# Attention units fed into an expert layer: x read back into the masks' ring, keys a step later, side work by an average

## The chip, the cores and the metric

One core of a Trainium2 chip runs the kernel. The metric is the device time of one execution, in microseconds; the time before is the median of three runs. Every duration below that isn't a run's time comes from one profiled execution.

## The reference

A gated linear attention over 4 batches, 8 heads, 768 positions and head size 48 is followed by two expert layers, all in f32:

```
f = sigmoid(f_logit)
state[t] = f[t] * state[t-1] + outer(k[t], v[t])       # per batch and head, 48 x 48
y[t] = q[t] @ state[t]
x = y as (3072, 384)
xn = x / sqrt(mean(x*x) + 1e-6) * rms_g
x3 = (silu(xn @ w_gate) * (xn @ w_val)) @ w_out         # 384 -> 1536 -> 384
out = relu(x3 @ w_in)**2 @ w2_out                       # 384 -> 2048 -> 384
```

## The kernel before

The attention is cut into 24 **units**: unit u is 128 positions of one batch, all 8 heads; `units` counts the batches first, so the state of a batch is needed again four units later. Four units make a group of 512 tokens, for which the first expert layer (`phase1`) runs once. Products in f32 are made of three matmuls each (`mm3`): an operand is split into a high and a low part ("h" and "l" in the names).

`first` computes units 0 to 7 and the expert layer of group 0 in an order written out by hand. Then `phase1` runs groups gi = 1 to 5. A group has 12 hidden blocks f, and each has three **steps**: a G step (9 matmuls for the gate, tile `g`), a V step (9 for the value, tile `v`) and an O step (9 of the output product of the block before, tiles `acc`). Step s of the whole stage is 36 gi + 3 f + 0, 1 or 2. With the G step ACT computes the silu (`si`, tile `sg`), with the V step DVE multiplies v into `sg` (`vs`) and ACT makes the high part `hh`, with the O step DVE makes the low part `hl`. `g` and `v` have one bank of PSUM each.

During the steps of group gi the units of group gi + 1 are prepared. `segment(s)` issues, after the matmuls of step s, first the functions of the dictionary `side` at s, then the step's own work (`si`; `vs` and `hh`; or `hl`), then the PE functions of `tail` at s. Each engine runs its instructions in the order in which they were issued. `plan_unit(u, s)` puts the parts of unit u at offsets from its start s:

- `load_gates`, `load_v`, `load_qk` ask for the unit's inputs on SP. `gate` (ACT, L296 and L297) makes sigmoids of the gates; `scan_b` (DVE, L308 and L309) and `scan_a` (DVE, L316) their running products; `mul_k` (L319) and `mul_q` (L322) multiply them into keys and queries.
- `scores` (PE, L341, tile `sc`) needs both products. `masked` (DVE, L360) writes the two masked tiles `sm`, from a ring of four buffers with the tag "sm", and `attend` (PE, L449 and L461) makes y from them and the state.
- `k_turn` (DVE, L395) transposes keys in blocks and stores them to memory (`kd`); `k_back` reads them back with their blocks swapped, `kcopy` (ACT, L436) copies them to `ktok`, `kv` (PE, L476) multiplies them with v, and `state_add` (DVE, L492) adds that to the state, which `decay` (ACT, L330) has scaled. Units 20 to 23 are the last of their batches and have none of these but `decay`.
- `norm` (ACT) and `power` (POOL) give the scale of the RMS norm, `x_scale` (DVE, L404) applies it, `x_turn` (DVE, L409) transposes in blocks and stores (`xd`, L383), `x_back` reads it back with four reads (L388), and `x_high` (ACT, L423) and `x_low` (DVE, L427) split it into `xh` and `xl`, the input of the group's G and V steps.

Beside that, the weights of the second expert layer are converted, summed and split (`w2_load`, `w2_scale`, `w2_bits`, `w2_sum`, `w2_part`, `w2_plain`) and stored to memory. `plan_work` puts these pieces into `side`, in their order, each into the first step in which DVE and ACT have room by the table `COST`: planned microseconds of a step may reach `CAP`, plus what `room` grants for the PE work of the attention in that step. In group 5, which has no units to prepare, the last weights are split, then `open_late` and `x3_load` (L1045) fetch weights and the first layer's results for the second layer (`phase2`), and `x_split` (ACT, L1086; DVE, L1087) and `x_sum` prepare them. The three copies of `acc` of a finished group (`evac_x3`, ACT, L903) take buffers of the tag "sm" too.

The ring of `qk` tiles has two buffers; a unit's x is read back into the place of its keys, so the buffer is held until `x_low`:

```
def x_back(u):
    block_read(u, "xd", block_view(U[u]["k"], KT))
```

Of the kernel before, what the change touches and what calls it, by code (L numbers as in the profile page):

```python
# [8 lines left out]
F32 = mybir.dt.float32  # L9
# [7 lines left out]
P = 128  # L17
# [5 lines left out]
KT = DM // P  # L23
# [4 lines left out]
UG = 4  # L28
# [161 lines left out]
def tile_linear_attention_moe(  # L190
# [16 lines left out]
    def pool(name, stack=main, **kw):  # L207
        return stack.enter_context(tc.tile_pool(name=name, **kw))
# [7 lines left out]
    ap_ = pool("attn", upper, bufs=2, reuse_waits="tile")  # L216
# [36 lines left out]
    def flat(x):  # L253
        return x.rearrange("p a t -> p (a t)")


    U = {}
# [117 lines left out]
    BL = 4  # L375

    def block_view(x, n):
        return flat(x)[:, 0:BL * n * 32].rearrange("p (b n j) -> p b n j", b=BL, n=n)
# [6 lines left out]
    def block_read(u, nm, to):  # L385
        src = U[u][nm].rearrange("(a i) c n j -> c i a (n j)", a=BL)
        for c in range(BL):
            nc.sync.dma_start(to[32 * c:32 * c + 32].rearrange("i a n j -> i a (n j)"), src[c])  # L388
        U[u][nm + "o"] = to
# [22 lines left out]
        block_write(u, "xd", t)  # L412

    def x_back(u):
        block_read(u, "xd", block_view(U[u]["k"], KT))

    def x_part(t, u):
        return t[:, :, u % UG * C:(u % UG + 1) * C].rearrange("p k (c i) -> p k c i", c=BL)
# [252 lines left out]
    def w2_plain(key, nm, a, b):  # L671
        if nm not in w2t:
            w2t[nm] = w2_tile(nm)
        w2_split(key, w2f[key], w2t[nm][:, a], w2t[nm][:, b])
# [37 lines left out]
    def w2_part(i, c):  # L712
        t, b = w2c[i, c]
        w2_split(("c", i, c), t[:, b], t[:, 2 + b], t[:, b])

    def w2_spare(i, key):
        t, _ = w2c[i, 2]
        w2_split(key, w2f[key], t[:, 1], t[:, 3])
# [31 lines left out]
    side, tail, planned, room = {}, {}, {}, {}  # L750
    TAIL = dict(scores=0.9, attend=1.3, kv=0.3)

    def at(where, s, fn):
        where.setdefault(max(s, NG), []).append(fn)

    starts = {}

    def plan_unit(u, s):
        starts[u] = s
        for k, fns in (  # L760
            (-9, (load_gates, load_v)), (max(-9, starts.get(u - 2, 0) + 10 - s), (load_qk,)), (-3, (gate,)), (-2, (scan_b, keep_end)), (-1, (scan_a, mul_k)),
            (0, (mul_q, k_turn, decay)), (1, (masked,)), (2, (k_back,)), (3, (norm, power)), (4, (kcopy, x_scale)),
            (5, (x_turn,)), (6, (state_add,)), (7, (x_back,)), (9, (x_high, x_low)),
        ):
            for fn in fns:
                if fn not in (load_gates, load_qk, load_v) or u > 2 * UG:
                    at(side, s + k, lambda fn=fn: fn(u))
                    planned.setdefault(s + k, []).append(fn.__name__)
        for k, fn in ((0, scores), (2, attend), (5, kv)):
            at(tail, s + k, lambda fn=fn: fn(u))  # L770
            room[s + k] = room.get(s + k, 0) + TAIL[fn.__name__]

    NG = 3 * F1
    for gi in range(1, NU - 1):
        for j in range(UG):
            plan_unit((gi + 1) * UG + j, gi * NG + ((4, 11, 19, 26) if gi == 1 else (-1, 8, 17, 26))[j])
    COST = dict(
        scan_b=(1.4, 0), keep_end=(0, 0.2), scan_a=(1.2, 0), mul_k=(0.7, 0), mul_q=(0.7, 0), masked=(1.4, 0),
        k_turn=(0.6, 0), kcopy=(0, 0.6), gate=(0, 2.2), decay=(0, 1.5), norm=(0, 1.0), x_scale=(0.5, 0), x_turn=(0.5, 0),
        state_add=(0.7, 0), x_high=(0, 0.5), x_low=(0.5, 0),  # L780
    )
    load = {}
    CAP = 2.1

    def busy(s):
        if s not in load:
            b = [(0.0, 0.6), (0.7, 0.6), (0.7, 0.0)][s % 3]
            load[s] = list(b)
        return load[s]

    for s, names in planned.items():
        for nm in names:
# [5 lines left out]
    def job(name, fn, dve=0.0, act=0.0, after=()):  # L798
        work.append((name, fn, (dve, act), after))

    def conversion(pair, after=()):
        job(("load", pair), lambda: w2_load(pair), after=after)

    def bits(pair, after=()):
        job(("scale", pair), lambda: w2_scale(pair), act=0.9, after=((("load", pair), 3),) + after)
        for n, c in enumerate((0.55, 0.96, 0.96)):
            job(("bits", pair, n), lambda n=n: w2_bits(pair, n), dve=c, after=((("scale", pair), 1),))

    def sums(i, cs, after=()):
        for n, x in enumerate(W_SUMS[cs]):  # L810
            act = x[1] == "="
            job(("sum", i, cs, n), lambda n=n: w2_sum(i, cs, n), dve=0 if act else 0.3, act=0.3 if act else 0, after=after)

    def split(name, fn, after=()):
        job(name, fn, dve=0.56, act=0.51, after=after)

    def plan_work():
        gone = ()
        for i in range(F2 // 3):
            a = tuple(("a", 3 * i + f) for f in range(3))  # L820
            b = tuple(("b", 3 * i + f) for f in range(3))
            pa, pb, pc = (a[0], a[1]), (a[2], b[0]), (b[1], b[2])
            if i == 0:
                conversion(pa)
                conversion(pb)
            bits(pa)
            bits(pb)
            sums(i, (0, 1))
            for c in (0, 1):
                split(("part", i, c), lambda i=i, c=c: w2_part(i, c), ((("sum", i, (0, 1), 5), 1),))  # L830
            sums(i, (2,))
            split(("part", i, 2), lambda i=i: w2_part(i, 2), ((("sum", i, (2,), 3), 1),))
            split(("plain", b[0]), lambda i=i, k=b[0]: w2_spare(i, k))
            sums(i, (3, 4), after=((("part", i, 1), 2),))
            conversion(pc, after=((("plain", b[0]), 2),))
            for c in (3, 4):
                split(("part", i, c), lambda i=i, c=c: w2_part(i, c), ((("sum", i, (3, 4), 5), 1),))
            bits(pc)
            if i + 1 < F2 // 3:
                na, nb = (("a", 3 * i + 3), ("a", 3 * i + 4)), (("a", 3 * i + 5), ("b", 3 * i + 3))  # L840
            else:
                na, nb = (("a", F2 - 1), ("b", F2 - 1)), None
            for n, k in enumerate(pc):
                split(("plain", k), lambda k=k, n=n, nm=f"b{3 * i + 1}": w2_plain(k, nm, 2 * n, 2 * n + 1))
                if n == 0:
                    conversion(na, after=((("bits", pc, 2), 1),))
            if nb:
                conversion(nb, after=((("plain", pc[1]), 2),))
        bits(na)
        for n, k in enumerate(na):  # L850
            split(("plain", k), lambda k=k, n=n: w2_plain(k, "last", 2 * n, 2 * n + 1))
        job(("open",), open_late, after=((("plain", na[1]), 1), (None, last0 + 2)))
        job(("x3",), lambda: (x3_tiles(), x3_load(0)), after=((None, last0 + 9),))
        freed = [2, 6, 8, 12, 14, 18, 20, 24, 26, 30, 32, 36]
        for n, p in enumerate(X_KEYS):
            f = next(f for f, c in enumerate(freed) if c >= n + 4)
            at_least = ((None, last0 + 3 * (f + 1) + 3), (("x3",), 3))
            for q in X_NEEDS.get(p, ()):
                job(("xsum", q), lambda q=q: x_sum(q, r_tile(f"xs_{q}")), dve=0.56, after=at_least)
            split(("x", p), lambda p=p: (x_tile(p), x_split(p)))  # L860
            work[-1] = work[-1][:3] + (at_least,)

        for b in range(10):
            f = next(f for f, c in enumerate(freed) if c >= b + 21)
            job(("b", b), lambda b=b: fetch_b(b), after=((None, last0 + 3 * (f + 1) + 3),))

        for name, fn, cost, after in work:
            s = max([NG, when.get("last", 0)] + [when[a] + g if a else g for a, g in after])
            while any(busy(s)[e] + c > CAP + room.get(s, 0) and c for e, c in enumerate(cost)):
                s += 1  # L870
            for e, c in enumerate(cost):
                busy(s)[e] += c
            when[name] = when["last"] = s
            at(side, s, fn)
# [161 lines left out]
    def x3_tiles():  # L1036
        L["x3"] = [wp.tile([P, 2, NT], F32, tag="w", name=f"x3_{k}") for k in range(KT)]

    def x3_load(s):
        o, g = 2 * NT * s, 0  # L1040
        while g < 2 * NT:
            gi, c = divmod(o + g, N)
            n = min(N - c, 2 * NT - g)
            for k in range(KT):
                nc.sync.dma_start(  # L1045
                    L["x3"][k].rearrange("p a t -> p (a t)")[:, g:g + n], x3d[gi][:, k, c:c + n]
                )
            g += n
# [374 lines left out]
```

## Time and profile before

| what | value |
|---|---|
| median of three runs | 980.8 us (979.37 to 981.16) |
| the profiled execution's own time | 979.5 us |
| its span, first to last instruction | 977.7 us |
| PE busy | 927.1 us, 95% |
| DVE busy | 646.3 us, 66% |
| ACT busy | 489.4 us, 50% |
| POOL busy | 31.6 us, 3% |
| mean granted clock of TensorE | 0.989 |

The span has four stretches: units 0 to 7 and group 0 of the first layer (to about 134 us), groups 1 to 4 with the units of groups 2 to 5 (to about 520 us), group 5 (to about 600 us), and the second layer. In the second layer PE is busy throughout. The start of a row is counted from the span's start.

### The profile page before, as it was taken

What the parts mean: (1) busy time and instruction counts of PE and PEld (TensorE: products, weight loads), DVE (VectorE), ACT (ScalarE), POOL (GpSimd) and SP (SyncE); (2) the same over time, 40 slices, a digit from 0 to 9 for tenths busy, and PEclk for the clock granted to TensorE, in tenths of its full rate; (3) what the DMA queues carried; (4) which work ended last, traced back from release to release, by engine and by line L of the source; (5) the groups of instructions that cost most, each with busy time, mean ns of one, the idle gap of its engine ahead of it and who ended that gap; (6) DMA issues with size and microseconds to landing.
All of it is one profiled execution on the core that took longest, in us unless ns stands there. A gap on an engine that the chain in (4) does not pass through costs nothing.

```text
span 977.7 us, 15776 instructions
## 1 busy us (share of the span) xinstructions
PE 927.1 (95%) x5945; PEld 813.0 (83%) x5945; DVE 646.3 (66%) x1147; ACT 489.4 (50%) x1020; POOL 31.6 (3%) x54
## 2 busy tenths in 40 slices
PE   6799999999899999998999799999999999999997
PEld 4578877877777777776777688999999999999997
DVE  6899967676666676765665354767675767667552
ACT  5877653444443544443434233556554655555451
POOL 3210000000000000000000000000000000000000
PEclk8999999999999999999999999999999999999999
DMA  9556443466456457446234425842464165406400
GB/s 322 181 184 209 150 165 103 122 195 187 130 170 220 133 175 230 123 150 208 75 114 162 178 97 184 287 141 75 137 194 148 39 206 159 146 12 182 129 25 28
DMA packets 78387, 148.48 MB, mean 152 GB/s; under 512 B 17248, under 2 KB 44000, under 8 KB 78304
## 3 DMA queue, kind: packets, MB, share of 16 engines
q1 hardware_dynamic: 78304, 147.39, 46.6%
q8 instruction: 49, 0.80, 0.3%
q14 instruction: 34, 0.28, 0.1%
HBM read 115.12 MB, written 32.24 MB: 151 GB/s over the span
## 4 chain that ended last, share of the span: by engine, by line
PE 87%; issue 3%; DMA 2%; DVE 2%; ACT 2%; SPq 0%; ACTq 0%; DVEq 0%
PE o L730 7%; PE o L729 7%; PE o L728 7%; PE X L1099 7%; PE Y L1099 5%; PE acc L728 5%; PE g L728 5%; PE g L729 5%; PE g L730 5%; PE acc L729 5%; PE acc L730 5%; PE v L728 5%; PE v L730 4%; PE v L729 4%; PE sc L341 2%
## 5 line engine op out<-in xcount | busy, mean ns | idle before, releaser
L730 PE MATMUL o<-wb,h 128*128 128x384 f32 x384 | 128.6, 335 | 0.0
L728 PE MATMUL o<-wb,h 128*128 128x384 f32 x384 | 128.3, 334 | 0.0
L729 PE MATMUL o<-wb,h 128*128 128x384 f32 x384 | 128.3, 334 | 0.0
L968 ACT CAST hh<-sg 128x512 fp32r<-128x512 f32 x72 | 44.6, 619 | 108.5 <-DVE sg L965 108.4
L960 ACT ACTIVATE sg<-g 128x512 f32<-128x512 f32 x72 | 42.7, 594 | 97.9 <-PE g L730 97.8
L965 DVE TENSOR_TENSOR sg<-v,sg 128x512 f32<-128x512 f32 x72 | 49.5, 688 | 61.2 <-PE v L730 60.8
L1099 PE MATMUL X<-xc,wa 128*128 128x384 f32 x360 | 82.5, 336 | 0.0
L730 PEld LDWEIGHTS o<-wb,h 128*128 128x128 f32 x384 | 72.1, 188 | 0.5
L728 PEld LDWEIGHTS o<-wb,h 128*128 128x128 f32 x384 | 72.1, 188 | 0.0
L729 PEld LDWEIGHTS o<-wb,h 128*128 128x128 f32 x384 | 72.1, 188 | 0.0
L1099 PE MATMUL Y<-xc,wa 128*128 128x384 f32 x300 | 68.3, 335 | 0.0
L1099 PEld LDWEIGHTS X<-xc,wa 128*128 128x128 f32 x360 | 63.8, 188 | 1.8 <-ACT d L1174 1.2
L1178 DVE TENSOR_TENSOR c<-T,c 128x384 f32<-128x384 f32 x40 | 22.3, 558 | 52.8 <-PE T L1099 43.6
L970 DVE TENSOR_TENSOR hl<-sg,hh 128x512 fp32r<-128x512 f32 x72 | 49.2, 683 | 10.2 <-ACT hh L968 9.8
L1099 PEld LDWEIGHTS Y<-xc,wa 128*128 128x128 f32 x300 | 53.3, 188 | 0.7 <-DVE c L1178 0.6
L728 PE MATMUL g<-xh,wh_o 128*128 128x512 f32 x108 | 45.2, 419 | 6.0 <-ACT sg L960 6.0
L1129 DVE TENSOR_TENSOR h<-d,h 128x384 fp32r<-128x384 f32 x60 | 32.8, 554 | 26.2 <-ACT h L1128 25.9
L341 PE MATMUL sc<-qk 64*128 64x128 f32 x320 | 23.5, 285 | 26.2 <-issue 25.1
L341 PEld LDWEIGHTS sc<-qk 64*128 64x128 f32 x320 | 20.0, 188 | 33.5 <-issue 31.9
L1128 ACT CAST h<-d 128x384 fp32r<-128x384 f32 x60 | 30.2, 511 | 34.4 <-PE o L730 34.4
L1174 ACT COPY d<-X 128x384 f32<-128x384 f32 x40 | 19.1, 478 | 54.7 <-PE X L1099 54.7
L728 PE MATMUL acc<-hh,wh_o 128*128 128x512 f32 x108 | 44.0, 407 | 0.0
(192 smaller groups left out, 2286.9 us busy)
## 6 DMA issues: line engine op xcount, KB each, us to landing
wa<-w2d_c SPq DMA_DIRECT2D x100, 384.0 KB, 3.4
raw<-in_w_dram SPq DMA_DIRECT2D x18, 768.0 KB, 4.3
ff<-in_ff_dram SPq DMA_DIRECT2D x20, 516.0 KB, 4.6
qk<-in_qk_dram SPq DMA_DIRECT2D x20, 512.0 KB, 5.9
w2d_c<-ws_c SPq DMA_DIRECT2D x50, 192.0 KB, 4.5
raw_a<-in_w_dram SPq DMA_DIRECT2D x22, 384.0 KB, 4.2
wb<-w2d_b SPq DMA_DIRECT2D x16, 384.0 KB, 3.6
v<-in_vp_dram SPq DMA_DIRECT2D x24, 192.0 KB, 4.5
```

Of the source, the lines that this page charges most:

```text
L341: nc.tensor.matmul(U[u]["sc", hf][:, j], U[u]["k"][o:o + 64, j], U[u]["q"][o:o + 64, j], start=True, stop=True,)
L728: nc.tensor.matmul(o, lh, rh, start=first, stop=False)
L729: nc.tensor.matmul(o, lh, rl, start=False, stop=False)
L730: nc.tensor.matmul(o, ll, rh, start=False, stop=last)
L960: nc.scalar.activation(dd["s", f], dd["g", f], AF.Silu)
L965: nc.vector.tensor_mul(dd["s", f], dd["v", f], dd["s", f])
L968: nc.scalar.copy(dd["h", f][0], dd["s", f])
L970: nc.vector.tensor_sub(dd["h", f][1], dd["s", f], dd["h", f][0].bitcast(F32))
L1099: nc.tensor.matmul(o, w[a], x[:, b], start=first and n == 0, stop=last and n == 2, skip_group_check=True,)
L1128: nc.scalar.copy(t[:, 0], r)
L1129: later(lambda: nc.vector.tensor_sub(t[:, 1], r, t[:, 0].bitcast(F32)))
L1178: nc.vector.tensor_add(t, bk[b], t)
```

## The change

`x_back` reads into a tile of its own, the ring "sm" of the masks, one step earlier (start + 6 instead of + 7), and `x_high` and `x_low` use it one step later (+ 10 instead of + 9). `kcopy` moves from + 4 to + 5, `kv` from + 5 to + 6, `state_add` from + 6 to + 7. `load_v` and `load_qk` are bound to the start of the unit two before (+ 7 and + 9), whose buffers they take. The starts of the units move: in group 1 to 4, 11, 18, 24 (from 4, 11, 19, 26), in groups 2 to 4 to -3, 6, 15, 24 (from -1, 8, 17, 26). Some costs of the planner's table are changed by 0.05 to 0.1, `CAP` goes from 2.1 to 2.3, and `crowd` is new: a piece of side work is put into a step only if no six steps in a row that hold it pass 6 x 2.05 us plus their room.

```diff
     def x_back(u):
-        block_read(u, "xd", block_view(U[u]["k"], KT))
+        block_read(u, "xd", ap_.tile([P, BL, KT, 32], F32, tag="sm", name=f"xo{u}", bufs=4))
...
         for k, fns in (
-            (-9, (load_gates, load_v)), (max(-9, starts.get(u - 2, 0) + 10 - s), (load_qk,)), (-3, (gate,)), (-2, (scan_b, keep_end)), (-1, (scan_a, mul_k)),
-            (0, (mul_q, k_turn, decay)), (1, (masked,)), (2, (k_back,)), (3, (norm, power)), (4, (kcopy, x_scale)),
-            (5, (x_turn,)), (6, (state_add,)), (7, (x_back,)), (9, (x_high, x_low)),
+            (-9, (load_gates,)), (max(-9, starts.get(u - 2, 0) + 7 - s), (load_v,)),
+            (max(-9, starts.get(u - 2, 0) + 9 - s), (load_qk,)),
+            (-3, (gate,)), (-2, (scan_b, keep_end)), (-1, (scan_a, mul_k)),
+            (0, (mul_q, k_turn, decay)), (1, (masked,)), (2, (k_back,)), (3, (norm, power)), (4, (x_scale,)),
+            (5, (x_turn, kcopy)), (6, (x_back,)), (7, (state_add,)), (10, (x_high, x_low)),
         ):
...
-        for k, fn in ((0, scores), (2, attend), (5, kv)):
+        for k, fn in ((0, scores), (2, attend), (6, kv)):
...
-            plan_unit((gi + 1) * UG + j, gi * NG + ((4, 11, 19, 26) if gi == 1 else (-1, 8, 17, 26))[j])
+            plan_unit((gi + 1) * UG + j, gi * NG + ((4, 11, 18, 24) if gi == 1 else (-3, 6, 15, 24))[j])
...
-    CAP = 2.1
+    CAP, MEAN = 2.3, 2.05
...
+    def crowd(s, e):
+        near = [(sum(busy(t)[e] for t in range(b, b + 6)), sum(room.get(t, 0) for t in range(b, b + 6))) for b in range(s - 5, s + 1)]
+        return max(n - r - 6 * MEAN for n, r in near)
...
-            while any(busy(s)[e] + c > CAP + room.get(s, 0) and c for e, c in enumerate(cost)):
+            while any(c and (busy(s)[e] + c > CAP + room.get(s, 0) or crowd(s, e) + c > 0) for e, c in enumerate(cost)):
                 s += 1
```

What this does to the order shows around unit 19. First DVE, before: from `scan_b` of unit 19 to its `k_turn`. L965 is `vs`, L970 `hl`, L427 `x_low` of unit 18, L322 `mul_q` of unit 19.

```order
L308 SCALAR_TENSOR_TENSOR ff19_3817<-ff19_3817,floor_89 128x516
L309 RECIPROCAL seed_90<-ff19_3817 128x4
L316 SCALAR_TENSOR_TENSOR ff19_3817<-ff19_3817,seed_90 128x516
L319 TENSOR_TENSOR qk19_3846<-qk19_3846,ff19_3817 128x512
L965 TENSOR_TENSOR sg_3_8_4004<-v_3_8_4006,sg_3_8_4004 128x512
L427 TENSOR_TENSOR xl_1_4_3555<-qk18_3597,xh_1_4_3554 128x3x128
L322 TENSOR_TENSOR qk19_3846<-qk19_3846,ff19_3817 128x512
L395 STREAM_TRANSPOSE ff19_3817<-qk19_3846 128x4x4x32
```

And now, on the same engine, to the first mask of unit 19 (`vs` is L971 here, `hl` L976):

```order
L492 TENSOR_TENSOR state2_99<-kv18_3965,state2_99 48x4x48 x2
L308 SCALAR_TENSOR_TENSOR ff19_3788<-ff19_3788,floor_89 128x516
L309 RECIPROCAL seed_90<-ff19_3788 128x4
L971 TENSOR_TENSOR sg_3_7_3963<-v_3_7_3974,sg_3_7_3963 128x512
L316 SCALAR_TENSOR_TENSOR ff19_3788<-ff19_3788,seed_90 128x516
L319 TENSOR_TENSOR qk19_3792<-qk19_3792,ff19_3788 128x512
L976 TENSOR_TENSOR hl_3_7_3993<-sg_3_7_3963,hh_3_7_3992 128x512
L322 TENSOR_TENSOR qk19_3792<-qk19_3792,ff19_3788 128x512
L395 STREAM_TRANSPOSE ff19_3788<-qk19_3792 128x4x4x32
L561 TENSOR_SCALAR m_a9_3989<-m_a9_3989 128x768
L568 SCALAR_TENSOR_TENSOR m_a9_3989<-raw_a9_3902,m_a9_3989 128x768
L427 TENSOR_TENSOR xl_1_4_3587<-xo18_3953,xh_1_4_3586 128x3x128
```

`mul_q` stood behind the next `vs` and the `x_low` of unit 18; now `vs` comes two instructions sooner, `hl` stands between, and `x_low` has gone behind `mul_q`, reading the new tile xo18.

PE around the scores of unit 19 before: they follow the nine matmuls of an O step.

```order
L728 MATMUL acc_3_2_3490<-hh_3_7_3959,wh_v7_1055 128x512
L729 MATMUL acc_3_2_3490<-hl_3_7_3960,wh_v7_1055 128x512
L730 MATMUL acc_3_2_3490<-hh_3_7_3959,wl_v7_1056 128x512
L341 MATMUL sc19_0_4046<-qk19_3846 128x128
L341 MATMUL sc19_1_4047<-qk19_3846 128x128
```

And now, on PE: they follow the nine of the next G step.

```order
L728 MATMUL g_3_8_4007<-xh_1_3_2653,wh_g8_1062 128x512
L729 MATMUL g_3_8_4007<-xl_1_3_2654,wh_g8_1062 128x512
L730 MATMUL g_3_8_4007<-xh_1_3_2653,wl_g8_1063 128x512
L341 MATMUL sc19_0_4035<-qk19_3792 128x128
L341 MATMUL sc19_1_4036<-qk19_3792 128x128
```

Between the `vs` ahead of `mul_q` and the scores PE now has an O and a G step where it had an O step alone.

SP's queue round the returned x of unit 18, before: the store of x, a load of weights, the four reads.

```order
L383 DMA xd18_3953<-qk18_3597 128x384
L640 DMA raw_a11_3955<-in_w2_dram 128x768 x2
L388 DMA qk18_3597<-xd18_3953 32x4x96 x4
L383 DMA kd19_4035<-ff19_3817 128x512
L284 DMA ff20_4041<-in_ff_dram 128x1032
```

And now, on SP:

```order
L383 DMA xd18_3938<-qk18_3552 128x384
L388 DMA xo18_3953<-xd18_3938 32x4x96 x4
L640 DMA raw_a11_3960<-in_w2_dram 128x768 x2
L383 DMA kd19_4019<-ff19_3788 128x512
L284 DMA ff20_4025<-in_ff_dram 128x1032
```

The reads stand directly behind the store that they wait for, and the load of weights behind them.

## Rows read from the trace of the kernel before

**Rows 1.** The page: PE's busy time, share of the span and instructions.

```profile
PE 927.1 (95%) x5945; PEld 813.0 (83%) x5945; DVE 646.3 (66%) x1147; ACT 489.4 (50%) x1020; POOL 31.6 (3%) x54
```

**Rows 2.** Waits of PE, 130 to 600 us: total, times, longest.

```profile
PE sc L341 <- issue: 25.1, 14, 4.5
PE g L728 <- ACT sg L960: 5.2, 1, 5.2
PE sc L341 <- DVE qk L322: 1.2, 1, 1.2
```

**Rows 3.** The chain that ended last: start, length, what.

```profile
161.59 0.60 issue
...
200.85 0.60 issue
...
223.87 2.06 issue
...
442.32 4.45 issue
...
493.46 1.99 issue
```

**Rows 4.** Timeline of DVE, 389 to 399 us: start, length, instruction, idle before.

```profile
390.39 1.23 DVE L308 TENSOR_TENSOR_SCAN ff<-ff,floor 128x516 f32<-128x516 f32 x1 [1.46 <-ACT ff L297]
...
391.87 1.23 DVE L316 TENSOR_TENSOR_SCAN ff<-ff,seed 128x516 f32<-128x516 f32 x1
393.02 0.67 DVE L319 TENSOR_TENSOR qk<-qk,ff 128x512 f32<-128x512 f32 x1
393.72 0.69 DVE L965 TENSOR_TENSOR sg<-v,sg 128x512 f32<-128x512 f32 x1
395.51 0.56 DVE L427 TENSOR_TENSOR xl<-qk,xh 128x384 fp32r<-128x384 f32 x1 [1.10 <-ACT xh L423]
395.99 0.69 DVE L322 TENSOR_TENSOR qk<-qk,ff 128x512 f32<-128x512 f32 x1
...
397.34 0.65 DVE L970 TENSOR_TENSOR hl<-sg,hh 128x512 fp32r<-128x512 f32 x1
397.94 1.29 DVE L360 TENSOR_TENSOR sm<-sc,mask 128x512 f32<-128x512 f32 x2
```

**Rows 5.** Timeline of ACT, the same stretch.

```profile
394.44 0.62 ACT L968 CAST hh<-sg 128x512 fp32r<-128x512 f32 x1 [1.30 <-DVE sg L965]
394.97 0.51 ACT L423 CAST xh<-qk 128x384 fp32r<-128x384 f32 x1
```

**Rows 6.** Timeline of PE, the same stretch: V, O, scores of unit 19.

```profile
391.40 0.39 PE L728 MATMUL v<-xh,wh_g 128*128 128x512 f32 x1
...
393.44 0.39 PE L728 MATMUL acc<-hh,wh_v 128*128 128x512 f32 x1
...
396.78 1.16 PE L341 MATMUL sc<-qk 64*128 64x128 f32 x16 [1.14 <-issue]
```

**Rows 7.** Groups by line: busy us, mean ns | idle before.

```profile
L492 DVE TENSOR_TENSOR state<-kv,state 48x192 f32<-48x192 f32 x32 | 11.2, 350 | 0.6 <-PE kv L476 0.4
...
L903 ACT COPY x3o<-acc 128x512 f32<-128x512 f32 x18 | 10.4, 588 | 7.2 <-PE acc L730 4.8 <-PE acc L1265 1.6
```

**Rows 8.** Timeline, 300 to 305 us: first G and first V matmul.

```profile
300.86 0.79 PE L728 MATMUL g<-xh,wh_o 128*128 128x512 f32 x1
...
304.56 0.39 PE L728 MATMUL v<-xh,wh_v 128*128 128x512 f32 x1
```

**Rows 9.** Timelines of ACT and PE, 535 to 560 us.

```profile
551.05 0.51 ACT L1086 CAST xc<-x 128x384 fp32r<-128x384 f32 x1 [9.23 <-DMA x<-x3d]
...
553.71 0.80 PE L728 MATMUL g<-xh,wh_o 128*128 128x512 f32 x1 [5.19 <-ACT sg L960]
```

**Rows 10.** DMA issues (count, KB, us to landing), and waits of SP.

```profile
raw_a<-in_w_dram SPq DMA_DIRECT2D x22, 384.0 KB, 4.2
...
xd<-qk SPq DMA_DIRECT2D x16, 192.0 KB, 1.9
qk<-xd SPq DMA_DIRECT2D x64, 48.0 KB, 2.8
...
SPq L388 <- DMA xd<-qk: 12.7, 6, 5.2
```

More of the change, by code (lines that the diff above doesn't have):

```diff
@@ L775, in tile_linear_attention_moe @@
         for j in range(UG):
-            plan_unit((gi + 1) * UG + j, gi * NG + ((4, 11, 19, 26) if gi == 1 else (-1, 8, 17, 26))[j])
+            plan_unit((gi + 1) * UG + j, gi * NG + ((4, 11, 18, 24) if gi == 1 else (-3, 6, 15, 24))[j])
     COST = dict(
         scan_b=(1.4, 0), keep_end=(0, 0.2), scan_a=(1.2, 0), mul_k=(0.7, 0), mul_q=(0.7, 0), masked=(1.4, 0),
-        k_turn=(0.6, 0), kcopy=(0, 0.6), gate=(0, 2.2), decay=(0, 1.5), norm=(0, 1.0), x_scale=(0.5, 0), x_turn=(0.5, 0),
-        state_add=(0.7, 0), x_high=(0, 0.5), x_low=(0.5, 0),
+        k_turn=(0.7, 0), kcopy=(0, 0.6), gate=(0, 2.2), decay=(0, 1.5), norm=(0, 1.0), x_scale=(0.6, 0), x_turn=(0.6, 0),
+        state_add=(0.7, 0), x_high=(0, 0.5), x_low=(0.55, 0),
     )
     load = {}
-    CAP = 2.1
+    CAP, MEAN = 2.3, 2.05
     def busy(s):
```

## The prediction

> **What bounds the kernel now.** Read the page first: PE is busy for 927.1 of the 977.7 us [rows 1], so an edit that takes nothing from PE's waits takes nothing from the time. Next read who made PE wait in the first expert stage, 130 to 600 us, where all the moved steps lie: three rows [rows 2]. The scores matmuls (L341) waited 25.1 us in 14 pieces that the profile calls "issue" and 1.2 us once for DVE's q product; G (L728) waited once for 5.2 us on ACT. The chain of waits shows the pieces [rows 3]: two of 0.60 (units 9 and 11), then one per unit from unit 12 (2.06) to unit 23 (1.99), the longest 4.45 (unit 21). Those twelve are 25.1 - 1.2 = 23.9 us. The 1.2 us is unit 8; unit 10 has no wait.
>
> What "issue" hides is read from the timelines round unit 19. A step of PE is nine matmuls, 2.04 us (391.40 to 393.44) [rows 6]. The next step begins at 393.44, and V's last matmul, 0.39 us long, ends some 0.15 after that. DVE then runs sg (393.72), ACT hh (394.44) and xh of the unit before (394.97), DVE xl (395.51, after 1.10 us of waiting for xh), and only then the q product, 395.99 to 396.68 [rows 4, 5]; the scores start at 396.78 [rows 6]. PE had one O step to fill, 2.05 us, and the series on DVE and ACT took 3.2: hence 1.14. That is the floor of all twelve; what is above it is DVE or ACT being behind already (scan_b of this unit began only when the gate came, after a wait of 1.46 [rows 4]).
>
> **The change, part by part.** Time below runs from the end of the last V step before a unit's scores.
>
> 1. *The scores move from an O step to a G step, xl from ahead of the q product to behind it.* The starts are now multiples of three, so PE has O and G between that V and the scores: 2 x 2.05 = 4.10 us. On DVE stand sg, scan_a, k product, hl, q product, and no xl. Rows 4 give 0.69, 1.23, 0.67, 0.65 and 0.69 us; instructions that wait for nothing start some 0.07 before the listed end of the one ahead (391.87 + 1.23 against 393.02). So 0.2 (V's last column and the semaphore) + 0.62 + 1.16 + 0.60 + 0.60 + 0.69 = 3.87, and 0.08 more until PE starts: 3.95. PE is there at 4.10: **no wait, with 0.15 to spare**. hl's hh is ready: ACT needs 0.62 from sg's end [rows 5], while DVE is in scan_a.
>
> 2. *Is DVE free when V ends?* The kv step now ends the G step three before the scores, then come state_add (2 x 0.35 [rows 7]) and scan_b with its reciprocal (1.4): 2.1 us in a V step of 2.05, if the gate is there when state_add ends. The gate (2.2 us on ACT by the planner's cost) follows hh and the key copy in the O step and begins about when its G step does, so it ends 1.1 us before state_add does. Free, just so.
>
> 3. *Exceptions.* The first unit of groups 2 to 4 now starts three steps before the group. ACT's three copies of acc (0.59 each [rows 7]) then stand ahead of the second unit's gate, some 1.7 us. That eats the 1.1: scan_b and all behind it come 0.2 late for units 13 and 17, and 0.5 for unit 21, which has no kv step in PE's way. Together 0.9. Unit 8 keeps its plan and its 1.2. Unit 9 has the key copy behind its gate instead of ahead: 0.6 earlier, its wait goes. Unit 11, six steps after unit 10, keeps 0.2 of 0.60.
>
> 4. *Masks, in the step after the scores.* From the scores' start DVE has the transposed keys (0.64), two pieces of side work (up to 1.5), xl (0.5) and the two masks (1.29 [rows 4]): done at 3.9. PE does the scores (1.16), V and O before it needs them, 5.25. Covered by 1.3. xl's xh follows the silu of the G step and is ready at 1.3, before DVE gets there.
>
> 5. *Returned x.* The store of x stands on SP behind the transpose, a step before the read now, and SP waits between: a store lands 1.9 us after issue, a read 2.8 [rows 10]. The four reads go out some 4 us after the transpose and have landed 3.6 us before xh asks for them. Behind SP's wait stands in many units one weight load, asked for four steps later; at 4.2 us to landing [rows 10] it has about 2.6 to spare. Both cost nothing. The page on SP's waits shows six such waits, 12.7 us in all, the longest 5.2 [rows 10]. The Trainium skill, page DMA: Bandwidth & Descriptors, section Anatomy of one DMA, puts a fixed 2.0 us on a DMA of the GpSimd path and most of it on the write's receipt, and says that with HBM as target this can be surprisingly long. By the rows the sum has 0 here; by that sentence the delay becomes the third rival. The trace has both, a median of 1.9 and a wait of 5.2.
>
> 6. *The tile from the masks' ring.* Four buffers now serve two masks, the returned x and the three x3o of a group. A buffer comes round after four takers; the one that held x is asked for nine steps after its last reader, and x3o of a group is stored five steps before the next mask. No wait. The qk tile is free once the key copy is done, so its load no longer waits for xl on SP; it was not late for PE, so 0.
>
> 7. *Keys, kv and state one step later*: the state is next read 36 steps on, 0. *Side work*: the same instructions; its last conversion ends one step sooner.
>
> 8. *The clock.* After the wait at unit 15 the nine G matmuls took 3.70 us (300.86 to 304.56) where they take 2.04: the first of them 0.79 long instead of 0.39, the lower of the two clock levels, 1.2 for 2.4 GHz [rows 8, 6]. The same follows unit 21's wait; I take the same price. 2 x 1.66 = 3.3 us come back with the waits. Not every wait cost it, so it could be 0 to 3.3; without the two longest I take all.
>
> 9. *The wait at 553 us.* ACT stood 9.23 us for x3 (551.05) with the silu behind it; G began at 553.71 after 5.19 of idleness [rows 9]. The loads hang on the last weight split, which gets 0.5 us earlier against PE; one more x sum and split crowd the steps behind it, about 0.3. Net 0.2; between -2 (a second wait behind the crowd) and +2 (one step sooner in full).
>
> **Sum.** Twelve units 23.9 - 0.9, units 9 and 11 0.6 + 0.4, clock 3.3, x3 0.2: 27.5 us. The profiled execution took 979.5 us (span 977.7), so **952.0**. The median of the runs shown is 980.8, 1.3 above it; I leave that in the range. The unknown is the margin of 0.15: from both sides, a unit's wait is at least 0 and at most the old floor of 1.14 (13.7 for twelve). I take 0 with the exceptions, since the chain is added from rows of the same instructions in the same queue.
>
> **Rivals.**
> - *The scores still wait, less.* DVE reaches V's end late, through gate, state_add or a piece of side work. For: points 1 and 2 have margins of 0.15 and nothing. Against: light steps of DVE (0 to 0.6 us planned) stand just ahead of state_add, so lateness doesn't add up. At 0.8 us a unit, 12 x 0.8 - 0.9 = 8.7 us more: 961. Chance 0.14.
> - *The change doesn't do what it says: the wait moves to attend.* Masks late behind xl and side work. It needs 1.3 us to show and 1.3 + 2.1 in every unit to eat the gain: about 979. Cap plus room allow 3.2 us of side work on DVE in the scores' step, so it is not excluded. Chance 0.03.
> - *Slower: x returns late.* xh now stands on ACT and xl on DVE ahead of the masks. If the read lands over 3.6 us later than in point 5, DVE stops before the masks, and PE at attend after 1.3 more. Break-even is 27.5 / 15 units = 1.8 beyond that, 6.7 us late each time; at 8 us late the 15 units cost 46 us: 998. SP once waited 5.2 for such a store, against a median of 1.9 to landing [rows 10], so one unit may come near, not all. Chance 0.03. The sentence of the Trainium skill in point 5 (DMA: Bandwidth & Descriptors) would speak for this rival.
>
> **How the numbers follow.** The forecast has 0.80; its own range is 948 (x3's 2 us and half the exceptions better) to 958 (half of the old floor at half the units, one clock drop left). Taking the first rival in up to 961 leaves out less than 2 in 10; below, 947 takes in the same gains with 1 us of the spread between runs. A difference of over 0.2% (2 us, what runs of this kernel can tell) on the fast side: 0.80 + 0.14 = 0.94; same 0.03; slower 0.03.
>
> **What would show it.** The row "sc waited" falls from 25.1 + 1.2 to about 2.3, unit 8 the largest; xl's wait for xh on DVE (1.10 at unit 19) goes; the scores of a unit follow a G step at once; no G matmul over 0.6 us between 130 and 520; the wait near 553 stays at about 5 us, some 27 us sooner; the second expert stage is as long as before. Wrong would be sc waits of 0.5 or more at most units (margin gone), y waiting (masks), ACT waiting for DMA at xh (late x), or a longer stretch from the x3 wait to the end.

## The result, and the profile after

The changed kernel took 955.4 us (median of four runs, 951.6 to 957.0), against 980.3 for the kernel before on the same chip: a ratio of 0.974, 95% interval 0.971 to 0.977. The forecast was 952.0. The profiled execution happened to be the shortest of the four, 951.6 us. Its page begins so; PE's busy time stands beside [rows 1]:

```profile
span 949.7 us, 15747 instructions
...
PE 923.9 (97%) x5945; PEld 813.3 (86%) x5945; DVE 644.6 (68%) x1147; ACT 488.5 (51%) x1020; POOL 31.4 (3%) x54
```

The span fell by 28.0 us and PE's busy time by 3.2: what went is waiting, and a little slow clock. PE's waits from 100 to 620 us (total, times, longest), to be read against [rows 2]:

```profile
PE g L728 <- ACT sg L966: 4.8, 1, 4.8
PE sc L341 <- DVE state L492: 2.6, 1, 2.6
PE sc L341 <- DVE qk L322: 1.2, 1, 1.2
PE v L728 <- DVE sg L971: 0.2, 1, 0.2
```

The row of 25.1 us and 14 pieces is gone. Unit 8's 1.2 is as before, and there is a new wait of 2.6, for the sum of the state (L492). The wait on ACT near the load of x3, the first layer's results (the expectations call it the third part of x), is still there, 4.8 where it was 5.2.

Round unit 19, DVE's timeline (start, length, instruction, idle before) shows the new series, to be read against [rows 4]:

```profile
369.65 0.72 DVE L492 TENSOR_TENSOR state<-kv,state 48x192 f32<-48x192 f32 x2 [2.51 <-PE kv L476]
370.41 1.23 DVE L308 TENSOR_TENSOR_SCAN ff<-ff,floor 128x516 f32<-128x516 f32 x1
371.67 0.18 DVE L309 RECIPROCAL seed<-ff 128x4 f32<-128x4 f32 x1
371.98 0.69 DVE L971 TENSOR_TENSOR sg<-v,sg 128x512 f32<-128x512 f32 x1
372.58 1.22 DVE L316 TENSOR_TENSOR_SCAN ff<-ff,seed 128x516 f32<-128x516 f32 x1
373.73 0.67 DVE L319 TENSOR_TENSOR qk<-qk,ff 128x512 f32<-128x512 f32 x1
374.31 0.69 DVE L976 TENSOR_TENSOR hl<-sg,hh 128x512 fp32r<-128x512 f32 x1
374.91 0.69 DVE L322 TENSOR_TENSOR qk<-qk,ff 128x512 f32<-128x512 f32 x1
...
377.70 0.55 DVE L427 TENSOR_TENSOR xl<-xo,xh 128x384 fp32r<-128x384 f32 x1
378.17 1.28 DVE L360 TENSOR_TENSOR sm<-sc,mask 128x512 f32<-128x512 f32 x2
```

And PE's, of the same stretch: the first and the last matmul of G, then the scores, with no idle time listed.

```profile
373.75 0.39 PE L728 MATMUL g<-xh,wh_g 128*128 128x512 f32 x1
...
375.56 0.39 PE L730 MATMUL g<-xh,wl_g 128*128 128x512 f32 x1
375.88 1.16 PE L341 MATMUL sc<-qk 64*128 64x128 f32 x16
```

Nothing on DVE waits between `scan_b` and the q product, which ends at 375.60, just ahead of PE. The split of the returned x, which cost 1.10 us of waiting ahead of the q product [rows 4], has gone behind it.

### The profile page after: what moved, and what is told of

It reads as the page before. It is cut to its first block, busy times and chain, and to the rows that moved or that the text cites. A ratio compares the mean times of both kernels' runs of the same rounds, so it can differ in the third digit from the quotient of the medians.

```text
span 949.7 us, 15747 instructions
## 1 busy us (share of the span) xinstructions
PE 923.9 (97%) x5945; PEld 813.3 (86%) x5945; DVE 644.6 (68%) x1147; ACT 488.5 (51%) x1020; POOL 31.4 (3%) x54
## 4 chain that ended last, share of the span: by engine, by line
PE 89%; DVE 3%; DMA 2%; ACT 1%; issue 0%; SPq 0%; ACTq 0%; DVEq 0%
PE o L730 7%; PE o L728 7%; PE o L729 7%; PE X L1105 7%; PE Y L1105 6%; PE v L728 5%; PE g L728 5%; PE acc L728 5%; PE v L730 5%; PE v L729 5%; PE acc L730 5%; PE acc L729 5%; PE g L730 5%; PE g L729 5%; PE sc L341 2%; PE T L1105 2%
## 5 line engine op out<-in xcount | busy, mean ns | idle before, releaser
L971 DVE TENSOR_TENSOR sg<-v,sg 128x512 f32<-128x512 f32 x72 | 49.5, 688 | 54.4 <-PE v L730 52.3
L976 DVE TENSOR_TENSOR hl<-sg,hh 128x512 fp32r<-128x512 f32 x72 | 49.3, 685 | 7.8 <-ACT hh L974 7.8
L728 PE MATMUL v<-xh,wh_v 128*128 128x512 f32 x108 | 43.8, 406 | 0.2 <-DVE sg L971 0.2
L728 PE MATMUL v<-xh,wh_g 128*128 128x512 f32 x108 | 43.9, 406 | 0.0
L728 PE MATMUL g<-xh,wh_g 128*128 128x512 f32 x108 | 43.6, 404 | 0.0
```

The source lines that it names most:

```text
L728: nc.tensor.matmul(o, lh, rh, start=first, stop=False)
L971: nc.vector.tensor_mul(dd["s", f], dd["v", f], dd["s", f])
L976: nc.vector.tensor_sub(dd["h", f][1], dd["s", f], dd["h", f][0].bitcast(F32))
```

## The experiments

All medians are of four runs, except the plan alone (ten). The kernel before, run beside them, gave 979.3 us with experiments 1 to 4, 983.4 with 5 to 8 and 979.3 with 9 and 10; each ratio is to its own. The three sets ran on different chips, so medians of different sets compare to some 4 us only; ratios, and stretches within the profiles, are the better measure. In the expectations, e5 is experiment 5, and so on. PE's waits are of 100 to 620 us in each profile.

**1. The changed kernel again, unedited.** The first four runs spread over 5.3 us, much for a kernel whose terms are fixed.

> The changed kernel, run again. Theory A (the scores' wait went because the q product now has an O and a G step of PE, 4.10 us, for a series of 3.95 on DVE, and x's low part no longer stands in front): the scores wait 0 to 0.3 us at units 12 to 23, 1.2 at unit 8, 2.6 at unit 11; time 951 to 957. If the margin of 0.15 us is what spreads the runs of this kernel (951.6 to 957.0), a profile of a slower run shows small waits of the scores at several units, 3 to 5 us in all. Rival (the spread is something else): no such waits, and the time is lost in another stretch.

It gave 955.4 us (954.1 to 956.2; ratio 0.974, 0.970 to 0.977). No unit from 12 to 23 waited in either profile, so a small margin that fails now and then isn't the cause. Two other things differ. Unit 6's scores began at 96.11 us here and at 94.12 in the first profile, all of it in the part that the change doesn't touch. And the two executions part after unit 11's wait. PE in the first profile:

```profile
193.51 0.56 PE L476 MATMUL kv<-v,ktok 128*48 128x48 f32 x16
194.01 0.48 PE L341 MATMUL sc<-qk 64*128 64x128 f32 x2
197.09 1.13 PE L341 MATMUL sc<-qk 64*128 64x128 f32 x14 [2.60 <-DVE state L492]
198.15 0.50 PE L728 MATMUL v<-xh,wh_g 128*128 128x512 f32 x1
...
200.32 0.39 PE L728 MATMUL acc<-hh,wh_v 128*128 128x512 f32 x1
```

And in this one:

```profile
195.49 0.56 PE L476 MATMUL kv<-v,ktok 128*48 128x48 f32 x16
195.99 0.48 PE L341 MATMUL sc<-qk 64*128 64x128 f32 x2
199.07 2.04 PE L341 MATMUL sc<-qk 64*128 64x128 f32 x14 [2.60 <-DVE state L492]
201.04 0.79 PE L728 MATMUL v<-xh,wh_g 128*128 128x512 f32 x1
201.63 0.63 PE L729 MATMUL v<-xl,wh_g 128*128 128x512 f32 x1
...
205.05 0.63 PE L728 MATMUL acc<-hh,wh_v 128*128 128x512 f32 x1
```

The wait is the same 2.60. From its end to the first matmul of O is 3.23 us there (197.09 to 200.32) and 5.98 here (199.07 to 205.05): here the clock fell to the lower of its two levels, 1.2 GHz, behind the wait. With 0.2 for the O matmul that is still slow, it cost 3.0 us more.

What PE waits for shows on DVE, in the first profile:

```profile
193.12 0.68 DVE L322 TENSOR_TENSOR qk<-qk,ff 128x512 f32<-128x512 f32 x1
193.84 0.71 DVE L395 STREAM_TRANSPOSE ff<-qk 128x512 f32<-128x512 f32 x1
194.47 0.51 DVE L665 TENSOR_TENSOR ws_c<-ws_c 128x384 fp32r<-128x384 f32 x1
...
196.23 0.72 DVE L492 TENSOR_TENSOR state<-kv,state 48x192 f32<-48x192 f32 x2
```

Unit 11's q product ends at 193.80, in time. But kv of unit 10 (start 18, plus 6) and the scores of unit 11 (start 24) are now in one step, and `banks` gives both the same PSUM bank: "pb" takes the kv tile and the scores' second half. The scores can't write it until `state_add` has read kv, and that is issued a step later, behind the transpose of keys, two split pieces and three sums. So PE stops after the first of the unit's eight matmuls (the profile lists each of them twice), ahead of the first that writes "pb", until the sum ends at 196.95. The program says the same: the first matmul into sc11_1 waits for the `state_add` of unit 10, and sc11_1 lies in the bank of kv10.

**2. The move of x alone,** in the kernel before: its starts, keys and planner stay.

```diff
-        block_read(u, "xd", block_view(U[u]["k"], KT))
+        block_read(u, "xd", ap_.tile([P, BL, KT, 32], F32, tag="sm", name=f"xo{u}", bufs=4))
...
-            (5, (x_turn,)), (6, (state_add,)), (7, (x_back,)), (9, (x_high, x_low)),
+            (5, (x_turn,)), (6, (x_back, state_add)), (9, (x_high, x_low)),
...
-                    at(side, s + k, lambda fn=fn: fn(u))
+                    at(side, s + k + (fn in (x_high, x_low) and s % NG != 26), lambda fn=fn: fn(u))
```

> The kernel before with x alone moved: read into the masks' ring at start + 6, its split issued one step later (but for the last unit of a group), all side work at its old places. Theory A: for units 13, 14, 15, 17, 18, 19, 21, 22, 23 the series sg, hh, xh, xl, q product (2.96 us) shortens to sg, q product (1.31); each wait falls by at least its floor of 1.14, 9 x 1.14 = 10.3 us or more; units 12, 16, 20 keep theirs; time 960 to 970. Theory B (the crowding of DVE by side work made the waits, and its averaging took them away): side work is as before, so the waits stay near 24 us and the time within 2 us of 980.

960.4 us (ratio 0.980, 0.976 to 0.984). Its waits:

```profile
PE sc L341 <- issue: 8.3, 8, 2.7
PE g L728 <- ACT sg L960: 4.5, 1, 4.5
PE sc L341 <- DVE qk L322: 1.2, 1, 1.2
```

Eight pieces and 8.3 us are left of 14 and 25.1; units 12, 16 and 20, ahead of whose q product the split stayed, keep 1.14, 1.14 and 1.39. So x alone gives 18.9 us where the whole change gives 23.9 beside it (979.3 to 955.4): what held the q product back was the split ahead of it. It isn't a share of the whole, though: in experiment 4 the rest of the change gives 15.9 with the split still in front (979.3 to 963.4). Either one takes out most of the same waits; the new starts by themselves were not tried.

**3. The planner alone:** new costs, cap and average in the kernel before.

```diff
-    CAP = 2.1
+    CAP, MEAN = 2.3, 2.05
...
+            while any(c and (busy(s)[e] + c > CAP + room.get(s, 0) or crowd(s, e) + c > 0) for e, c in enumerate(cost)):
```

> The kernel before with the planner's part alone: the new costs, CAP 2.3, the average over six steps; starts, x and keys as before. By its table the last weights are split some eight steps earlier, so the x3 wait of 5.2 us and its slow matmuls (1.7) should go in any case. Theory A: each of units 12 to 23 keeps at least the floor of 1.14, so the scores wait 14 to 24 us; time 963 to 974. Theory B: the scores' waits fall below 6 us; time under 955.

975.6 us in ten runs (ratio 0.996, 0.994 to 0.999). The expectation missed: the waits of scores did not fall.

```profile
PE sc L341 <- issue: 27.1, 14, 3.6
PE sc L341 <- DVE qk L322: 1.2, 1, 1.2
```

What fell away is the wait for x3: no row of ACT stands here. In this plan the last weights are split eight steps sooner, and the load of x3, whose own step is the same, goes out on SP at 534.73 us instead of 541.91. The placement of side work was not what made the scores late, then.

**4. The low part of x ahead of the q product,** in the changed kernel: the point on which the forecast's margin rests, tried directly.

```diff
-                    at(side, s + k, lambda fn=fn: fn(u))
+                    at(side, s + k - (fn in (x_high, x_low)), lambda fn=fn: fn(u))
```

> The changed kernel with x's split issued one step earlier again (start + 9, ahead of the next unit's q product), all else, side work included, at its place. Theory A: xl's 0.48 us stands in the series, 3.95 + 0.48 = 4.43 against PE's 4.10, so units 12 to 23 wait about 0.3 each, 3 to 5 us in all (more where xh has to wait for x to land); time 955 to 961. Theory B: no scores' wait above 0.1, time as the changed kernel.

963.4 us (ratio 0.983, 0.979 to 0.987), a little above what was expected. The waits of scores that the changed kernel hasn't:

```profile
PE sc L341 <- issue: 4.3, 2, 2.3
PE sc L341 <- PE g L730: 2.9, 10, 0.7
```

DVE round unit 19:

```profile
384.48 0.55 DVE L427 TENSOR_TENSOR xl<-xo,xh 128x384 fp32r<-128x384 f32 x1
384.95 0.69 DVE L322 TENSOR_TENSOR qk<-qk,ff 128x512 f32<-128x512 f32 x1
```

And PE, from the first matmul of G to the scores:

```profile
383.31 0.39 PE L728 MATMUL g<-xh,wh_g 128*128 128x512 f32 x1
...
385.74 1.16 PE L341 MATMUL sc<-qk 64*128 64x128 f32 x16 [0.22 <-PE g L730]
```

From the start of the G step the q product ends after 2.33 us here and 1.85 in the changed kernel, 0.48 later; the scores start after 2.43 (383.31 to 385.74) and 2.13 (373.75 to 375.88), 0.30 later. **The margin is 0.18**, where 0.15 had been worked out. (The listed 0.22 is shorter than 0.30 since it counts from the listed end of G's last matmul, which the scores of the changed kernel overlap.) The two pieces of over 2 us are units 13 and 17, where xl also waits for xh, and ACT for the returned x (2.75 and 2.95 us): a step sooner it has not landed there. In the changed kernel neither waits, because xl no longer stands in front.

**5. Unit 11 one step later,** in the changed kernel, so that kv of unit 10 is a step ahead of its scores.

```diff
-            plan_unit((gi + 1) * UG + j, gi * NG + ((4, 11, 18, 24) if gi == 1 else (-3, 6, 15, 24))[j])
+            plan_unit((gi + 1) * UG + j, gi * NG + ((4, 11, 18, 25) if gi == 1 else (-3, 6, 15, 24))[j])
```

> The changed kernel with one edit: unit 11 starts at step 25 instead of 24, so that kv of unit 10 (step 24) and the scores of unit 11 no longer fall in one step and no longer need the same PSUM bank pb within it. Nothing is left out of the computation. Theory A (unit 11's wait of 2.6 us comes from that bank, held until state_add of unit 10): the wait sc<-DVE state is gone, at most 0.5 us of waits of scores is left beside unit 8's 1.2, and the time is 2.6 us (5.6 where the clock fell after it) below the changed kernel's 955.4: 949.5 to 953. Rival B (scores of unit 11 wait for a late q product or for the state as such, not for the bank): a wait of 1 us or more stays at unit 11, time 954 to 957.

952.0 us (950.1 to 953.0; ratio 0.969, 0.966 to 0.971). The row of the state is gone. The edit moves the scores and not the bank; with the program's wait (experiment 1) it shows the bank as the cause.

```profile
PE g L728 <- ACT sg L966: 5.9, 2, 5.7
PE sc L341 <- DVE qk L322: 1.1, 1, 1.1
```

**6. The second layer's split later:** at least six steps behind its load.

```diff
-            at_least = ((None, last0 + 3 * (f + 1) + 3), (("x3",), 3))
+            at_least = ((None, last0 + 3 * (f + 1) + 3), (("x3",), 6))
```

> The changed kernel with one edit: the first piece of the x split of the second layer is placed at least 6 steps, not 3, behind the load of its third part. Nothing is left out. Theory A (the wait of 4.8 us at 525 us comes from a transfer that has not landed when ScalarE asks for it, and costs its own 4.8 us and about 2 us more of slow matmuls behind it): the wait is under 1 us, time 947 to 950. Rival B (the later pieces are then late themselves for the second part of the kernel, which starts a step later): PE waits 2 to 5 us at the start of the second layer instead, time 953 to 957.

950.6 us (948.9 to 952.4; ratio 0.967, 0.964 to 0.970). In the changed kernel ACT stood 8.80 us for the load and PE 4.76 behind it:

```profile
521.91 0.51 ACT L1092 CAST xc<-x 128x384 fp32r<-128x384 f32 x1 [8.80 <-DMA x<-x3d]
```

Here ACT still stands, but only 2.55, and nothing that PE needs is behind it:

```profile
526.27 0.51 ACT L1092 CAST xc<-x 128x384 fp32r<-128x384 f32 x1 [2.55 <-DMA x<-x3d]
```

PE's rows: 1.5 in two pieces on ACT and 0.2 on hl, the first some 11 us behind that, in place of 4.8.

```profile
PE g L728 <- ACT sg L966: 1.5, 2, 1.0
...
PE acc L729 <- DVE hl L976: 0.2, 1, 0.2
```

**7. The keys back where they were,** one step earlier, the rest as changed.

```diff
-                    at(side, s + k, lambda fn=fn: fn(u))
+                    at(side, s + k - (fn in (kcopy, state_add)), lambda fn=fn: fn(u))
...
-            at(tail, s + k, lambda fn=fn: fn(u))
+            at(tail, s + k - (fn is kv), lambda fn=fn: fn(u))
```

> The changed kernel with the keys put back: kcopy, kv and state_add of each unit are issued one step earlier, as in the kernel before; starts, x, ring, costs and placement as in the changed kernel. Nothing is left out. Theory A (moving the keys gained nothing where DVE is free by then, and it is what put kv of unit 10 into the step of the scores of unit 11): units 12 to 23 wait for under 0.5 us in all, unit 11's wait falls from 2.6 to under 1, time 949 to 953. Rival B (DVE's copy of keys and state_add are in the way of the q product when they come a step sooner): 0.3 to 1 us of wait in each of 10 units, time 958 to 965.

952.2 us (950.7 to 953.2; ratio 0.969, 0.967 to 0.972). Unit 11's wait went here too, since kv of unit 10 is then in the step before; unit 9's 0.6 came back, and 0.4 is left at unit 11. Units 12 to 23 wait for nothing.

```profile
PE sc L341 <- issue: 0.6, 1, 0.6
PE sc L341 <- PE g L730: 0.4, 1, 0.4
```

**8. Experiments 5 and 6 together.**

```diff
-            plan_unit((gi + 1) * UG + j, gi * NG + ((4, 11, 18, 24) if gi == 1 else (-3, 6, 15, 24))[j])
+            plan_unit((gi + 1) * UG + j, gi * NG + ((4, 11, 18, 25) if gi == 1 else (-3, 6, 15, 24))[j])
...
-            at_least = ((None, last0 + 3 * (f + 1) + 3), (("x3",), 3))
+            at_least = ((None, last0 + 3 * (f + 1) + 3), (("x3",), 6))
```

> The changed kernel with the edits of e5 and e6 together (unit 11 a step later, x split at least 6 steps behind its load). Nothing is left out. Theory A (two separate waits, each worth its length and the slow matmuls behind it): both are gone, 2.6 to 5.6 and 5 to 7 us off 955.4, 943 to 948. Rival B (the time that one gives back is taken by the next late transfer): 950 to 955.

945.0 us (944.3 to 945.5; ratio 0.962, 0.959 to 0.964): faster than both kernels, and the four runs spread over 1.2 us where those of the changed kernel first spread over 5.3.

```profile
PE g L728 <- ACT sg L966: 1.5, 2, 1.0
PE sc L341 <- DVE qk L322: 1.2, 1, 1.2
PE acc L729 <- DVE hl L976: 0.5, 3, 0.2
```

**9. The old planner under the new starts,** x and keys (costs, cap and loop).

```diff
-    CAP, MEAN = 2.3, 2.05
+    CAP = 2.1
...
-            while any(c and (busy(s)[e] + c > CAP + room.get(s, 0) or crowd(s, e) + c > 0) for e, c in enumerate(cost)):
+            while any(busy(s)[e] + c > CAP + room.get(s, 0) and c for e, c in enumerate(cost)):
```

> The changed kernel with the planner of the kernel before: the old costs of six operations, a cap of 2.1 a step and no average over six steps; starts, x and keys as in the changed kernel. Nothing is left out. The last weights are then formed at step 196 and the third part of x is fetched at step 197 instead of 188. Theory A (the new place of x alone makes the scores free; the average does little): units 12 to 23 wait for at most 2 us in all, the x3 wait moves to about 546 us and lasts 3 to 9 us, time 952 to 962. Rival B (without the average DVE is full for several steps in a row and the q products come late): waits of scores of 5 us or more over units 12 to 23, time 962 to 972.

957.3 us (ratio 0.977, 0.974 to 0.980), about 2 us above the changed kernel. The scores of units 12 to 23 wait 0.6 in all, so the average isn't what frees them. x3 comes later and holds PE longer:

```profile
PE acc L729 <- DVE hl L972: 7.1, 1, 7.1
PE sc L341 <- DVE state L492: 2.3, 1, 2.3
...
PE kv L476 <- ACT ktok L436: 1.1, 1, 1.1
```

**10. Experiments 6 and 7 together.**

```diff
-                    at(side, s + k, lambda fn=fn: fn(u))
+                    at(side, s + k - (fn in (kcopy, state_add)), lambda fn=fn: fn(u))
...
-            at(tail, s + k, lambda fn=fn: fn(u))
+            at(tail, s + k - (fn is kv), lambda fn=fn: fn(u))
...
-            at_least = ((None, last0 + 3 * (f + 1) + 3), (("x3",), 3))
+            at_least = ((None, last0 + 3 * (f + 1) + 3), (("x3",), 6))
```

> The changed kernel with the edits of e6 and e7 together: keys one step earlier, as in the kernel before, and the x split at least 6 steps behind its load. Nothing is left out. Theory A (the later keys gain nothing; all they do is to put kv of unit 10 beside the scores of unit 11): as e8, 943.5 to 946.5, waits of scores of at most 2.5 us in all. Rival B (the earlier keys cost where the x pieces come later): 947 to 952, waits over 3 us.

947.3 us (946.6 to 947.8; ratio 0.968, 0.965 to 0.971), just inside what the second theory gave, with waits between the two: the scores wait 2.6 us in all (unit 8's 1.2, 0.6, and 0.8 in two). From unit 6's scores to the second layer's first matmul it takes 470.5 us, against 469.9 in experiment 8; most of the rest of the 2.3 between the medians, which are of different chips, lies in the first 96 us (unit 6 at 95.62 against 94.37), which the two share line by line. So the later keys, beside a start of 25 for unit 11, are worth about half a microsecond there at most, which these runs can't settle.

## Why the prediction was right, and where it was wrong

From the start of unit 6's scores to the first matmul of the second layer, which leaves out the first 96 us and what is the same in all, by PE's timelines of the profiles; PEclk is the granted clock in the 8 us behind unit 11's scores (198 to 206 us), from the view by stretches:

| kernel | us | PE's wait at unit 11 | its wait for x3 | PEclk |
|---|---|---|---|---|
| before | 502.0 | 0.6 | 5.2 | 1.00 |
| changed, first profile | 476.9 | 2.6 | 4.8 | 1.00 |
| changed again (1) | 479.7 | 2.6 | 4.5 | 0.57 |
| unit 11 later (5) | 475.1 | 0 | 5.7 | 1.00 |
| split later (6) | 473.7 | 2.6 | 1.5, later | 0.79 |
| keys back (7) | 474.8 | 0.4 | 4.5 | 1.00 |
| both (8) | 469.9 | 0 | 1.5, later | 1.00 |

- **Point 1, right, and the largest term.** Scores in a G step, xl behind the q product: waits gone at all twelve units. The margin is 0.18, for 0.15 worked out (experiment 4). Two of its terms were short by 0.08 and cancel: sg begins 0.28 behind the end of the V step by [rows 4, 6], not 0.2, and the G step takes 2.13 to the scores, not 2.05. x alone gave 19 us (experiment 2).
- **Point 2, right.** At unit 19 `state_add` begins at 369.65 and `scan_b` at 370.41 with no wait for the gate.
- **Point 3, wrong in both directions.** Units 13, 17 and 21 were to wait 0.9 together, and no wait is listed. At units 13 and 17 the gate does come 0.26 late to `scan_b`, as worked out; half of that is gone by sg, the margin takes the rest. Only unit 21's scores start later behind their G step, 2.29 instead of 2.13. Unit 8 and unit 9 came as said. **"Unit 11 keeps 0.2 of 0.60" is the step that failed**: 2.6, and 3.0 more where the clock fell behind it. I had followed DVE's queue to the q product and not asked which PSUM bank the scores write and who still reads it. The time of kv's move (point 7, "0") was looked up for the state and not for the bank. The Trainium skill, page Perfetto Trace Analysis, section Optimizing Tensor Performance, says that independent groups of matmuls should rotate through different PSUM banks, so that one is read while the next is written. Unit 11 is where this kernel did not; by the table experiment 5 takes 1.8 us less than the first profile of the changed kernel and 4.6 less than the second, though it waits some 1 us longer for x3.
- **Point 4, right.** At unit 19 the masks end at 379.45, 3.6 us after the scores' start at 375.88 (3.9 forecast); PE needs them at 5.25.
- **Point 5, right in what it cost, wrong in its room.** SP's waits for the store rose from 12.7 us in six [rows 10] to 35.8 in sixteen, the longest 5.1, since the read is directly behind it. ACT never waited for the returned x: the rival of the late read didn't come. But the 3.6 us of room aren't there in every unit. For unit 18 they are about 3 (last read issued at 371.5, 1.9 to landing, xh at 376.5). For unit 12 they are about 0.4 (240.0, 2.0 and 242.36): there SP stores x3 of the finished group ahead of x.
- **Point 7 for the keys, half right.** Moving them gave nothing at units 12 to 23 (experiment 7) and 0.6 at unit 9, and with the new starts it made unit 11's wait.
- **Point 8, right in its sign.** The two stretches of lower clock behind units 15 and 21 are gone, 3.3 us. They did not follow the two longest waits, as the forecast has it: behind unit 13's 2.73 no G matmul took over 0.5 us, behind unit 15's 2.41 seven took over 0.6. And behind the x3 wait twelve matmuls took over 0.6 us in the first profile, where it was six before: about 1.1 us back. Unit 11's wait had a new one behind it in the second profile, and a shorter one in those of experiments 4, 6 and 9.
- **Point 9, right.** 5.19 became 4.8 and 4.5, for a forecast net of 0.2.

The terms of the first profile: waits of scores 26.3 - 3.8 = 22.5, clock 3.3 - 1.1 = 2.2, x3 0.4: 25.1, and 2.0 from the first 96 us, by chance (unit 6's scores at 96.10 before, at 94.12 here), make 27.1 of the 28.0. In the second profile the 2.0 are missing and unit 11's slow clock takes 3.0. So the first run came below the forecast of 952.0 and the median 3.4 above it. With unit 11 a step later (experiment 5) the median is 952.0, as forecast, but that the two agree is luck: the kernel before took 983.4 beside it, and the forecast started from 979.5.

## What to carry to other kernels

When work is moved by a step, list for each moved matmul which PSUM bank it writes and which engine reads that bank last, beside the queues: a wait for a bank shows as a wait for an instruction that computes nothing the waiting matmul needs. Put what the critical operation doesn't need behind it in its queue, here one 0.55 us split and its 1.10 us of waiting: that was worth more than any balance of the side work. And price a wait with the slow matmuls that may follow it: by the rows PE waits 5.6 us less in experiment 8 than in the first profile of the changed kernel, and the table gives 7.0 us less; against the second profile, where the clock fell behind unit 11, it is 9.8.

## What the runs showed of the chip that I had not expected

- **The same wait may or may not cost the clock.** Behind the 2.6 us (2.3 in experiment 9) at unit 11 the granted clock from 198 to 206 us was 1.00 in one profile and 0.57 in another of the same kernel, 0.79 in experiments 4, 6 and 9; in experiments 5, 7, 8 and 10, where PE stood there for 0.4 at most, it was 1.00. What decides it stays open.
- **The stretch of low clock has no fixed length.** Twelve matmuls of the first profile, and seven of the second, took over 0.6 us behind x3 waits of 4.8 and 4.5.
- **The first 96 us vary by 3 us between profiles of the same code there**, with unit 6's scores at 94.1 to 97.0. For that reason alone a difference of 3 us can't be read from a single run.
